# Starting the FFN on two batches and re-timing loads in a fused retention and SwiGLU kernel

## The chip, the cores and the metric

One core of one Trainium2 chip. The metric is the device time of one execution in microseconds. The profile's span is about 1.7 us shorter than that time. TensorE is called PE in the profile, its weight loads PEld, VectorE DVE, ScalarE ACT, GpSimd POOL, SyncE SP. SPq is SyncE's sequencer, which does nothing here but issue DMAs. The "landing" of a DMA is the moment its data has arrived; landing times are counted from the start of the issue. A line of a timeline holds start, length, engine, line, operation, output and input.

## The reference, cut to what matters

Retention attention over 4 batches, 8 heads, 768 positions, head size 64, then RMS norm and a SwiGLU FFN (512 to 1536 to 512) over the 3072 tokens.

```
for t in range(S):                       # retention
    state = gamma * state + k[t] v[t]^T
    y[t]  = scale * q[t] state
xn  = x / sqrt(mean(x*x) + 1e-6) * rms_g # FFN
out = (silu(xn @ w_gate) * (xn @ w_val)) @ w_out
```

## The kernel before: the parts that matter

The positions are cut into 6 chunks of 128. FFN group c works on chunk c of all four batches (512 tokens), while the attention of chunk c+1 is woven into its slots: slots 0 to 11 are the gate and value products ("gv"), the later ones the down products ("down"). The order of the program is each engine's order; there is no scheduler.

In what follows, b is the batch, and xn is the normalised x of one batch and chunk; group c's first full product needs the transposes of all four xn of chunk c. For chunks 2 and later q, k and the normalised xn are transposed by DMA, all issued from SyncE:

```
def piece_t(c, b):                 # T: transposes of q and k
    if c > 1:
        for n in "qk":
            t = work.tile([128, NHP, 128], BF16, name=n + "T", bufs=8)
            nc.sync.dma_start_transpose(out=t, in_=d[n + "b"])
        return
    ...                            # chunks 0 and 1: on TensorE

def piece_n(c, b):                 # N: normalised x
    if c > 1:
        nc.vector.scalar_tensor_tensor(out=xn, in0=x, scalar=d["rstd"], in1=g_bc, ...)
        nc.sync.dma_start_transpose(out=cur[c, "xnT"][:, :, b * C:(b + 1) * C], in_=xn)
        return
    ...
```

The slots of a group, and what is done ahead for the chunk after next (L load, T transposes, V the product v times decay):

```
PLAN = dict(a=(5, 5, 9, 9), y=(7, 8, 11, 12), n=(9, 10, 13, 13))   # chunks 2..5
AHEAD = {1: ((L, 0),), 3: ((L, 1),), 5: ((L, 2),), 7: ((T, 0),), 8: ((T, 1),), 9: ((L, 3),), 11: ((T, 2),),
         13: ((V, 0),), 14: ((V, 1), (T, 3)), 15: ((V, 2), (V, 3))}
for c in range(NCH):
    for i, f_slot in enumerate(ffn(c)):
        f_slot()                          # gv(i), or down(b): 12 products, a copy, an output DMA on SyncE
        for f in a_slots[i]: f()          # the attention of chunk c+1, by PLAN
        ahead(c, i)                       # the work for chunk c+2, by AHEAD
```

Of the kernel before, what the change touches and what calls it, by code (L numbers as in the profile page):

```python
# [9 lines left out]
F32 = mybir.dt.float32  # L10
# [7 lines left out]
def kernel(  # L18
# [11 lines left out]
    nc = tc.nc  # L30
# [31 lines left out]
            nc.sync.dma_start(out=x, in_=src[0].rearrange("h (c p) d -> c p h d", p=C)[0])  # L62
            raw[name] = x

    def load(c, b):
        d = cur.setdefault((c, b), {})
        for name, src in (("qb", q), ("kb", k)):
            x = work.tile([128, DM], BF16, name=name, bufs=8)
            nc.gpsimd.dma_start(  # L69
                out=x.rearrange("p (h d) -> p h d", h=H),  # L70
                in_=src[b].rearrange("h (c p) d -> c p h d", p=C)[c])
            d[name] = x
        d["v_f"] = loads.tile([128, H, D], F32, name="v_f")
        nc.gpsimd.dma_start(out=d["v_f"], in_=v[b].rearrange("h (c p) d -> c p h d", p=C)[c])  # L74

    cur = {}
    load_first()
# [42 lines left out]
    nc.vector.memset(mhalf, -0.5)  # L120
    ident = const.tile([128, 128], BF16, name="ident")
    make_identity(nc, ident)
    for b in range(1, B):
        load(0, b)

    g_bc = const.tile([128, DM], F32, name="g_bc")
# [12 lines left out]
    wg_v = moe_w_gate.rearrange("(k p) n -> p k n", p=128)  # L139
    wv_v = moe_w_val.rearrange("(k p) n -> p k n", p=128)  # L140
    wo_v = moe_w_out.rearrange("(n p) m -> p n m", p=128)
    WB = ((0, 384), (384, 768), (768, DFF))

    def load_wg(i):
        sl = slice(*WB[i])
# [19 lines left out]
    def piece_c(b):  # L165
# [3 lines left out]
            copy(d[name], raw[name[0] + "_f"].rearrange("p h d -> p (h d)"))  # L169
        d["v_f"] = raw["v_f"]  # L170

    def piece_v(c, b):
        d = cur[c, b]
        d["vp"] = work.tile([128, H, D], BF16, name="vp", bufs=6)
        (nc.vector if c == 0 and b < 3 else nc.gpsimd).tensor_tensor(  # L175
            out=d["vp"], in0=d["v_f"], in1=vdec[:, c, :, None].to_broadcast([128, H, D]), op=ALU.mult)

    def piece_t(c, b):
# [37 lines left out]

    def piece_y(c, b):
        d = cur[c, b]
        pool, tag = (fps, "ff") if c == 0 else (aps, "at")
        y_ps = pool.tile([128, H, D], F32, name="y_ps", tag=tag)  # L220
        first = True
        for hp in range(NHP):
            for i in range(2):
                h = 2 * hp + i
                last = c == 0 and h == H - 1
                nc.tensor.matmul(y_ps[:, h, :], d["am"][:, i, hp, :], d["vp"][:, h, :],  # L226
                                 start=first, stop=last, skip_group_check=True)
                first = False
        if c > 0:
            for hp in range(NHP):  # L230
                nc.tensor.matmul(y_ps[:, 2 * hp:2 * hp + 2, :], d["qT"][:, hp, :], st_b[b][:, hp, :],  # L231
                                 start=False, stop=hp == NHP - 1, skip_group_check=True)
        if 0 < c < NCH - 1:
            kv_ps = piece_kv(c, b)
        x = y_ps if c == 0 else work.tile([128, H, D], F32, name="x", bufs=5)
        if c > 0:
            nc.vector.tensor_tensor(  # L237
                out=x, in0=y_ps, in1=ydec[:, c, :, None].to_broadcast([128, H, D]), op=ALU.mult)
        xsq = work.tile([128, DM], F32, name="xsq", bufs=1)
        ssq = work.tile([128, 1], F32, name="ssq")  # L240
        nc.scalar.activation(xsq, x.rearrange("p h d -> p (h d)"), AF.Square,  # L241
                             accum_out=ssq)
        d["ssq"] = ssq
        d["x"] = x
        if c == 0:
            return
        piece_rstd(c, b)
        if c < NCH - 1:
            nc.vector.tensor_tensor(out=st_f[b], in0=st_f[b], in1=kv_ps, op=ALU.add)
            piece_sb(b)  # L250

    def piece_kv(c, b):
        d = cur[c, b]
# [7 lines left out]
    def piece_s(b):  # L261
        nc.scalar.copy(st_f[b], piece_kv(0, b))

    def piece_sb(b):
        for i in range(2):
            r = slice(i * 64, i * 64 + 64)
            nc.gpsimd.tensor_copy(st_b[b][r, :, i * 64:i * 64 + 64], st_f[b][r, :, i * 64:i * 64 + 64])  # L267

    def piece_rstd(c, b):
        ms = work.tile([128, 1], F32, name="ms")  # L270
# [18 lines left out]
    def piece_x(c, b):  # L289
        d = cur[c, b] if c == 0 else cur.pop((c, b))  # L290
        if c > 1:
            return
        xn = d["xn"]
        xt_ps = aps.tile([128, KS, 128], BF16, name="xt_ps", tag="at")
        for s in range(KS):
            nc.tensor.transpose(xt_ps[:, s, :], xn[:, s * 128:(s + 1) * 128], ident)  # L296
        xnT = cur[c, "xnT"][:, :, b * C:(b + 1) * C]
        if c == 0 and b < 2:
            for s in range(KS):
                nc.scalar.activation(xnT[:, s, :], xt_ps[:, s, :], AF.Copy, scale=g_col[:, s:s + 1])  # L300
            return
        nc.vector.tensor_tensor(  # L302
            out=xnT, in0=xt_ps,
            in1=g_col[:, :, None].to_broadcast([128, KS, 128]), op=ALU.mult)
# [5 lines left out]

    PLAN = dict(a=(5, 5, 9, 9), y=(7, 8, 11, 12), n=(9, 10, 13, 13))

    PLAN1 = dict(v=(7, 9, 11, 14), t=(8, 10, 12, 15), a=(9, 11, 14, 17), y=(10, 13, 16, 19), n=(12, 15, 18, 21), x=(13, 17, 20, 22))

    def attention(c):
        s = [[] for _ in range(24 if c == 1 else 16)]
        s[0].append(lambda: begin(c))
        plan = PLAN1 if c == 1 else PLAN
        pieces = dict(v=piece_v, t=piece_t, a=piece_a, y=piece_y, n=piece_n, x=piece_x)
        for b in range(B):  # L320
            for n, slot in plan.items():
                s[slot[b]].append(lambda f=pieces[n], b=b: f(c, b))
        return s


    def ffn(c):
# [2 lines left out]
        slots = []  # L329


        def gv(n0, n1=None, t=slice(0, GT)):
            n1 = n0 + 1 if n1 is None else n1
            w = t.stop - t.start
            g_ps = fps.tile([128, n1 - n0, w], F32, name="g_ps", tag="ff")
            v_ps = fps.tile([128, n1 - n0, w], F32, name="v_ps", tag="ff")
            for ps, w_b in ((g_ps, wg_b), (v_ps, wv_b)):
                for n in range(n0, n1):
                    for s in range(KS):
                        nc.tensor.matmul(ps[:, n - n0, :], w_b[:, s, n * 128:(n + 1) * 128], xnT[:, s, t],  # L340
                                         start=s == 0, stop=s == KS - 1)
            sg = ffw.tile([128, n1 - n0, w], BF16, name="sg")
            nc.scalar.activation(sg, g_ps, AF.Silu)  # L343
            nc.vector.tensor_tensor(out=hT[:, n0:n1, t], in0=sg, in1=v_ps, op=ALU.mult)  # L344


        EARLY = 4
        early = slice(0, GT - C)

        def gv_first(n):  # L350
            gv(n, t=early)
            if n == 1:
                piece_x(0, B - 1)
            if n == EARLY - 1:
                gv(0, EARLY, slice(GT - C, GT))

        o_t = {}

# [22 lines left out]
            nc.sync.dma_start(out=out_v[c, b], in_=o_sb)  # L381

        for n in range(NFF):
            slots.append(lambda n=n: gv_first(n) if c == 0 and n < EARLY else gv(n))
        if c == 0:
            for i in range(3):
                for b in range(B):
# [11 lines left out]
    def warm_up(c, n):  # L399
        for i in range(n):  # L400
            nc.tensor.matmul(hot_ps, hot[:, 0:128], hot, start=True, stop=True)  # L401

    P = dict(C=lambda c, b: piece_c(b), V=piece_v, T=piece_t, A=piece_a, Y=piece_y,
             R=piece_rstd, N=piece_n, X=piece_x, G=lambda c, i: load_wg(i), U=lambda c, i: load_wv(i), H=warm_up)
    for step in ("H9 H8 C0 T0 H4 V0 A0 H4 V1 T1 H4 G0 Y0 R0 U0 H4 A1 V2 T2 H4 Y1 R1 G1 U1 H2 A2 N0 T3 Y2 R2 "
                 "X0 N1 H2 A3 X1 N2 H9 H6 X2 H3 V3 Y3 H6 G2 U2 R3 N3").split():
        P[step[0]](0, int(step[1]))
    make_causal()
    load(1, 0)

    L, T, V, W = load, piece_t, piece_v, lambda c, i: load_wo(i)
    AHEAD = {1: ((L, 0),), 3: ((L, 1),), 5: ((L, 2),), 7: ((T, 0),), 8: ((T, 1),), 9: ((L, 3),), 11: ((T, 2),),
             13: ((V, 0),), 14: ((V, 1), (T, 3)), 15: ((V, 2), (V, 3))}


    AHEAD0 = {2: ((L, -1, 1),), 4: ((W, 0),), 5: ((L, -1, 2),), 6: ((W, 1),), 8: ((L, -1, 3),), 9: ((W, 2), (L, 0)),
              11: ((L, 1),), 13: ((T, 0),), 14: ((L, 2),), 15: ((T, 1),), 19: ((T, 2), (L, 3))}
    LATE0 = {0: ((V, 0), (V, 1), (V, 2)), 1: ((T, 3),), 4: ((V, 3),)}

    def ahead(c, i):  # L420
        for f, *x in (AHEAD0 if c == 0 else AHEAD).get(i, ()) if c < NCH - 2 else ():
            f(c + 2 + sum(x[:-1]), x[-1])
        for f, b in LATE0.get(i, ()) if c == 1 else ():
            f(2, b)

    for c in range(NCH):
        f_slots = ffn(c)
        a_slots = attention(c + 1) if c + 1 < NCH else [[] for _ in range(16)]
        for i, f_slot in enumerate(f_slots):
            if i == NFF + 1 and c > 0:  # L430

                for f in a_slots[i]:
                    f()
                a_slots[i] = []
            f_slot()
            if c == 0 and i < B:
                piece_s(i)
                piece_sb(i)
            for f in a_slots[i]:
                f()  # L440
            ahead(c, i)
            if c == 0 and i == 22:
                nc.sync.dma_start(out=g_bc, in_=moe_rms_g.partition_broadcast(128))
# [1 line left out]
_INS = ['q', 'k', 'v', 'moe_w_gate', 'moe_w_val', 'moe_w_out', 'moe_rms_g']  # L445
# [26 lines left out]
```

## Time and profile before

| | before |
|---|---|
| time | 237.49 us (237.37 to 237.71, 3 runs) |
| first FFN product | 20.43 us |
| group 1 starts | 61.67 us |
| group 2 starts | 96.80 us |
| TensorE busy from 61.67 to 221.80 us | 159.07 of 160.13 us |

Here is SyncE's timeline in group 1 (start, length of the issue, engine, line, operation, output and input):

```profile
73.54 1.19 SPq L183 DMA_TRANSPOSE qT<-qb  x1
74.82 1.22 SPq L183 DMA_TRANSPOSE kT<-kb  x1
77.00 1.20 SPq L183 DMA_TRANSPOSE qT<-qb  x1
78.28 1.22 SPq L183 DMA_TRANSPOSE kT<-kb  x1
83.11 4.81 SPq L284 DMA_TRANSPOSE xnT<-xn  x2
88.02 1.22 SPq L183 DMA_TRANSPOSE qT<-qb  x1
89.33 1.22 SPq L183 DMA_TRANSPOSE kT<-kb  x1
90.64 1.09 SPq L381 DMA_DIRECT2D out_dram<-o_sb  x1
91.82 2.53 SPq L284 DMA_TRANSPOSE xnT<-xn  x2
```

Two pairs of q and k transposes are issued before the first xn is ready, and one pair stands between the second and the third transpose of xn. The answer for the last two transposes of xn, and TensorE's timeline where group 2 wants them:

```profile
DMA to landing us min/median/max: 2.5/2.5/2.5
```

```profile
96.80 1.03 PE L340 MATMUL g_ps<-xnT,wg_b 128*128 128x512 bf16 x4
```

The last of them lands at 95.61 us. So the kernel before had a margin of 1.2 us there, and no row of a page says so. VectorE had the third and fourth xn ready at 91.1 and 92.7 us, so each was issued within 0.8 us.

### The profile page before, as it was taken

To read this page: it belongs to the slowest core of one execution; us is meant where nothing else is said; L and a number is where in the kernel's file an instruction comes from. 1 tells how busy PE (TensorE), PEld (TensorE's weight loads), DVE (VectorE), ACT (ScalarE), POOL (GpSimd) and SP (SyncE) were. 2 spreads that over 40 slices of the span, in tenths; PEclk is the share of its full clock that TensorE was granted. 3 is DMA by queue.
4 is the path that set the end of the run, shared out by engine and by line. 5 is a ranking of instruction groups with operands and counts; after the bars stand their busy time and mean duration, and the time that the engine had idled before them with its cause. 6 is when DMAs were issued, how large, how long until landed. Compare 5 with 4: busy or idle time off the path is not lost.

```text
span 236.0 us, 4231 instructions
## 1 busy us (share of the span) xinstructions
PE 226.4 (96%) x1587; PEld 119.3 (51%) x1613; DVE 126.8 (54%) x212; ACT 88.9 (38%) x172; POOL 128.5 (54%) x198
## 2 busy tenths in 40 slices
PE   7979999999899999999999999999999999999994
PEld 4657744565345555445554445554445554444443
DVE  6585435678337794147794147794148582243300
ACT  7475544432433423333433333433332532433221
POOL 8978989887997458970458970559300202000000
PEclk9999999999999999999999999999999999999999
DMA  7999999999999998899099999695900025200022
GB/s 135 178 188 204 211 193 204 206 196 139 180 271 174 163 139 152 172 213 161 11 127 122 173 205 104 79 133 135 181 0 0 3 44 152 73 0 0 0 89 90
DMA packets 87956, 30.69 MB, mean 130 GB/s; under 512 B 78528, under 2 KB 83392, under 8 KB 87936
## 3 DMA queue, kind: packets, MB, share of 16 engines
q0 software_dynamic: 54432, 16.78, 70.9%
q1 hardware_dynamic: 32832, 13.51, 30.7%
q8 instruction: 12, 0.20, 0.4%
q10 hardware_dynamic: 672, 0.13, 0.3%
q14 instruction: 8, 0.07, 0.1%
HBM read 28.58 MB, written 6.29 MB: 148 GB/s over the span
## 4 chain that ended last, share of the span: by engine, by line
PE 85%; DVE 4%; ACT 4%; POOL 3%; issue 2%; ACTq 0%; DVEq 0%; POOLq 0%
PE g_ps L340 26%; PE v_ps L340 26%; PE o_ps L375 21%; PE a_ps L208 3%; PE y_ps L226 2%; PE hot_ps L401 2%; PE y_ps L231 2%; PE kv_ps L257 2%; DVE am L214 1%; DVE xn L286 1%; PE o_ps L365 1%; ACT xsq L241 1%; DVE x L237 1%; PE xt_ps L296 1%; POOL rstd L274 1%
## 5 line engine op out<-in xcount | busy, mean ns | idle before, releaser
L344 DVE TENSOR_TENSOR hT<-sg,v_ps 128x512 bf16<-128x512 bf16 (+1 forms) x73 | 49.5, 678 | 79.9 <-PE v_ps L340 70.0
L340 PE MATMUL v_ps<-xnT,wv_b 128*128 128x512 bf16 (+2 forms) x298 | 73.5, 368 | 0.4
L340 PE MATMUL g_ps<-xnT,wg_b 128*128 128x512 bf16 (+2 forms) x293 | 73.1, 368 | 0.5
L343 ACT ACTIVATE sg<-g_ps 128x512 bf16<-128x512 f32 (+1 forms) x73 | 43.0, 589 | 64.8 <-PE g_ps L340 62.4
L375 PE MATMUL o_ps<-wo_b,hT 128*128 128x512 bf16 x267 | 61.9, 379 | 0.5 <-issue 0.2
L340 PEld LDWEIGHTS <-wv_b 128*128 128x128 bf16 x304 | 29.1, 98 | 33.1
L340 PEld LDWEIGHTS <-wg_b 128*128 128x128 bf16 x304 | 27.7, 98 | 29.2 <-DVE xnT L302 0.4
L375 PEld LDWEIGHTS <-hT 128*128 128x128 bf16 x276 | 26.1, 98 | 28.7 <-DVE hT L344 0.2
L271 POOL TENSOR_SCALAR ms<-ssq 128x1 f32<-128x1 f32 x24 | 5.6, 232 | 62.3 <-ACT xsq L241 61.9
L241 ACT ACTIVATE xsq<-x 128x512 f32<-128x512 f32 x20 | 12.6, 630 | 35.1 <-DVE x L237 33.3
L214 DVE TENSOR_TENSOR am<-a_ps,causal 128x512 bf16<-128x512 f32 x40 | 24.9, 679 | 0.0
L380 ACT COPY o_sb<-o_ps 128x512 f32<-128x512 f32 x23 | 13.2, 581 | 29.3 <-PE o_ps L375 23.3
L69 POOL DMA_DIRECT2D qb<-in_q_dram x23 | 21.7, 944 | 0.4 <-DMA kb<-in_k_dram 0.3
L175 POOL TENSOR_TENSOR vp<-v_f,vdec 128x512 bf16<-128x512 f32 x21 | 21.5, 1042 | 0.5
L74 POOL DMA_DIRECT2D v_f<-in_v_dram x23 | 21.3, 924 | 0.1
L69 POOL DMA_DIRECT2D kb<-in_k_dram x23 | 20.7, 901 | 0.1
L267 POOL CAST st_b<-st_f 64x256 bf16<-64x256 f32 x40 | 18.1, 454 | 1.3
L237 DVE TENSOR_TENSOR x<-y_ps,ydec 128x512 f32<-128x512 f32 x20 | 13.7, 684 | 2.9 <-PE y_ps L231 2.9
L282 DVE SCALAR_TENSOR_TENSOR xn<-x,rstd,g_bc 128x512 bf16<-128x512 f32 x16 | 12.7, 791 | 3.5 <-POOL rstd L274 3.5
L274 POOL TENSOR_TENSOR rstd<-ms,mhalf 128x1 f32<-128x1 f32 x24 | 13.3, 555 | 2.0
L401 PE MATMUL hot_ps<-hot 128*128 128x256 bf16 x65 | 11.6, 329 | 1.1 <-DVE hot L93 1.1
L226 PEld LDWEIGHTS <-am 128*128 128x128 bf16 x192 | 8.8, 98 | 5.3 <-DVE am L214 0.9
(71 smaller groups left out, 145.5 us busy)
## 6 DMA issues: line engine op xcount, KB each, us to landing
v_f<-in_v_dram POOLq DMA_DIRECT2D x23, 256.0 KB, 7.3
out_dram<-o_sb SPq DMA_DIRECT2D x23, 256.0 KB, 2.3
qb<-in_q_dram POOLq DMA_DIRECT2D x23, 128.0 KB, 7.1
kb<-in_k_dram POOLq DMA_DIRECT2D x23, 128.0 KB, 6.8
wo_b<-in_moe_w_out_dram POOLq DMA_DIRECT2D x3, 512.0 KB, 9.7
wg_b<-in_moe_w_gate_dram POOLq DMA_DIRECT2D x2, 384.0 KB, 6.5
wv_b<-in_moe_w_val_dram POOLq DMA_DIRECT2D x2, 384.0 KB, 7.3
wg_b<-in_moe_w_gate_dram POOLq DMA_DIRECT2D x1, 768.0 KB, 8.6
```

The source lines that it names most:

```text
L69: nc.gpsimd.dma_start(out=x.rearrange("p (h d) -> p h d", h=H), in_=src[b].rearrange("h (c p) d -> c p h d", p=C)[c])
L74: nc.gpsimd.dma_start(out=d["v_f"], in_=v[b].rearrange("h (c p) d -> c p h d", p=C)[c])
L175: (nc.vector if c == 0 and b < 3 else nc.gpsimd).tensor_tensor(out=d["vp"], in0=d["v_f"], in1=vdec[:, c, :, None].to_broadcast([128, H, D] ...
L214: nc.vector.tensor_tensor(out=am[:, i], in0=a_ps[i], in1=mask, op=ALU.mult)
L237: nc.vector.tensor_tensor(out=x, in0=y_ps, in1=ydec[:, c, :, None].to_broadcast([128, H, D]), op=ALU.mult)
L267: nc.gpsimd.tensor_copy(st_b[b][r, :, i * 64:i * 64 + 64], st_f[b][r, :, i * 64:i * 64 + 64])
L274: nc.gpsimd.tensor_tensor(out=rstd, in0=ms, in1=mhalf, op=ALU.pow)
L340: nc.tensor.matmul(ps[:, n - n0, :], w_b[:, s, n * 128:(n + 1) * 128], xnT[:, s, t], start=s == 0, stop=s == KS - 1)
L343: nc.scalar.activation(sg, g_ps, AF.Silu)
L344: nc.vector.tensor_tensor(out=hT[:, n0:n1, t], in0=sg, in1=v_ps, op=ALU.mult)
L375: nc.tensor.matmul(o_ps, hT[:, n, b * C:(b + 1) * C], wo_b[:, n, :], start=n == 0, stop=n == NFF - 1)
L401: nc.tensor.matmul(hot_ps, hot[:, 0:128], hot, start=True, stop=True)
```

## The change

Its intent: start the FFN on two batches as soon as they are normalised, with the weights loaded ahead of the fourth batch; let group 1 start on three batches; take state copies and some products off GpSimd; load chunk 2 within group 0. The core of the diff (the head's order of steps and helper functions are cut, some lines joined, comments added):

```diff
-    WB = ((0, 384), (384, 768), (768, DFF))
+    WB = tuple((i * 384, (i + 1) * 384) for i in range(4))
+    VECTOR_V = ((0, 0), (0, 1), (0, 2), (1, 1), (1, 2), (1, 3))      # V on VectorE for these
-            piece_sb(b)
+            piece_sb(b, nc.gpsimd.tensor_copy if c > 1 else nc.scalar.copy)
+        def first(i):                       # group 0: two batches, then three, the fourth later
+            two, three, third, fourth = slice(0, 2 * C), slice(0, 3 * C), slice(2 * C, 3 * C), slice(3 * C, GT)
+            if i == 0:
+                gv(0, 2, two, lambda: piece_x(0, 2)); gv(2, 3, two); gv(0, 3, third)
+            elif i < 8:
+                gv(i + 2, t=three)
+            ...
+        def second(n):                      # group 1: three batches for its first two gates
+            gv(n, t=slice(0, GT - C))
+            ...
 ... (cut)
+    AHEAD0 = {1: ((L, 1, 1),), 5: ((W, 0, 0),), 6: ((L, 1, 2),), ...    # group 0: chunk 1, w_out, chunk 2
+              16: ((L, 2, 3, "qk"),), 17: ((L, 2, 3, "v"),), 23: ((T, 2, 2),)}
+    AHEAD1 = {0: ((V, 1, 0), (V, 1, 1), (V, 1, 2)), 1: ((T, 1, 3),), 3: ((V, 1, 3),),
+              4: ((L, 2, 0),), 6: ((L, 2, 1),), 8: ((L, 2, 2),), 9: ((T, 2, 0), (L, 2, 3)), 11: ((T, 2, 1),),
+              12: ((T, 2, 2),), 13: ((V, 2, 0),), 14: ((V, 2, 1), (T, 2, 3)), 15: ((V, 2, 2), (V, 2, 3))}
```

Group 1 gets a plan of its own, AHEAD1. Its second number is relative to the group, so (L, 2, 0) and (T, 2, 0) are chunk 3's batch 0. Against AHEAD, chunk 3's loads go from slots 1, 3, 5, 9 to 4, 6, 8, 9, and its transposes from 7, 8, 11, 14 to 9, 11, 12, 14.

More of the change, by code (lines that the diff above doesn't have):

```diff
@@ L63, in load_first, with load @@
             raw[name] = x
-    def load(c, b):
+    def load(c, b, parts="qkv"):
         d = cur.setdefault((c, b), {})
-        for name, src in (("qb", q), ("kb", k)):
-            x = work.tile([128, DM], BF16, name=name, bufs=8)
-            nc.gpsimd.dma_start(
-                out=x.rearrange("p (h d) -> p h d", h=H),
-                in_=src[b].rearrange("h (c p) d -> c p h d", p=C)[c])
-            d[name] = x
-        d["v_f"] = loads.tile([128, H, D], F32, name="v_f")
-        nc.gpsimd.dma_start(out=d["v_f"], in_=v[b].rearrange("h (c p) d -> c p h d", p=C)[c])
+        for n in parts:
+            if n == "v":
+                x = d["v_f"] = loads.tile([128, H, D], F32, name="v_f")
+            else:
+                d[n + "b"] = work.tile([128, DM], BF16, name=n + "b", bufs=8)
+                x = d[n + "b"].rearrange("p (h d) -> p h d", h=H)
+            nc.gpsimd.dma_start(out=x, in_=dict(q=q, k=k, v=v)[n][b].rearrange("h (c p) d -> c p h d", p=C)[c])
     cur = {}
@@ L122 @@
     make_identity(nc, ident)
-    for b in range(1, B):
+    for b in (1, 2):
         load(0, b)
@@ L174, in piece_v @@
         d["vp"] = work.tile([128, H, D], BF16, name="vp", bufs=6)
-        (nc.vector if c == 0 and b < 3 else nc.gpsimd).tensor_tensor(
+        (nc.vector if (c, b) in VECTOR_V else nc.gpsimd).tensor_tensor(
             out=d["vp"], in0=d["v_f"], in1=vdec[:, c, :, None].to_broadcast([128, H, D]), op=ALU.mult)
@@ L218, in piece_y @@
         d = cur[c, b]
-        pool, tag = (fps, "ff") if c == 0 else (aps, "at")
+        pool, tag = (fps, "ff") if c == 0 and b < B - 1 else (aps, "at")
         y_ps = pool.tile([128, H, D], F32, name="y_ps", tag=tag)
@@ L262, in piece_s, with piece_sb @@
         nc.scalar.copy(st_f[b], piece_kv(0, b))
-    def piece_sb(b):
+    def piece_sb(b, copy=nc.scalar.copy):
         for i in range(2):
             r = slice(i * 64, i * 64 + 64)
-            nc.gpsimd.tensor_copy(st_b[b][r, :, i * 64:i * 64 + 64], st_f[b][r, :, i * 64:i * 64 + 64])
+            copy(st_b[b][r, :, i * 64:i * 64 + 64], st_f[b][r, :, i * 64:i * 64 + 64])
     def piece_rstd(c, b):
@@ L297, in piece_x @@
         xnT = cur[c, "xnT"][:, :, b * C:(b + 1) * C]
-        if c == 0 and b < 2:
+        if (c, b) == (0, 0):
             for s in range(KS):
@@ L311 @@
     PLAN = dict(a=(5, 5, 9, 9), y=(7, 8, 11, 12), n=(9, 10, 13, 13))
-    PLAN1 = dict(v=(7, 9, 11, 14), t=(8, 10, 12, 15), a=(9, 11, 14, 17), y=(10, 13, 16, 19), n=(12, 15, 18, 21), x=(13, 17, 20, 22))
+    PLAN1 = dict(v=(9, 12, 14, 17), t=(9, 11, 13, 16), a=(10, 12, 15, 18), y=(11, 14, 17, 20),
+                 n=(13, 16, 19, 22), x=(15, 18, 21, None))
     def attention(c):
@@ L319, in attention @@
         pieces = dict(v=piece_v, t=piece_t, a=piece_a, y=piece_y, n=piece_n, x=piece_x)
-        for b in range(B):
-            for n, slot in plan.items():
-                s[slot[b]].append(lambda f=pieces[n], b=b: f(c, b))
+        for n, slot in plan.items():
+            for b in range(B):
+                if slot[b] is not None:
+                    s[slot[b]].append(lambda f=pieces[n], b=b: f(c, b))
         return s
@@ L329, in ffn, with gv @@
         slots = []
-        def gv(n0, n1=None, t=slice(0, GT)):
+        def gv(n0, n1=None, t=slice(0, GT), between=None):
             n1 = n0 + 1 if n1 is None else n1
@@ L337, in gv @@
             for ps, w_b in ((g_ps, wg_b), (v_ps, wv_b)):
+                if between is not None and ps is v_ps:
+                    between()
                 for n in range(n0, n1):
@@ L344, in gv @@
             nc.vector.tensor_tensor(out=hT[:, n0:n1, t], in0=sg, in1=v_ps, op=ALU.mult)
-        EARLY = 4
-        early = slice(0, GT - C)
-        def gv_first(n):
-            gv(n, t=early)
-            if n == 1:
-                piece_x(0, B - 1)
-            if n == EARLY - 1:
-                gv(0, EARLY, slice(GT - C, GT))
+        def first(i):
+            two, three, third, fourth = slice(0, 2 * C), slice(0, 3 * C), slice(2 * C, 3 * C), slice(3 * C, GT)
+            if i == 0:
+                gv(0, 2, two, lambda: piece_x(0, 2))
+                gv(2, 3, two)
+                gv(0, 3, third)
+            elif i < 8:
+                gv(i + 2, t=three)
+            else:
+                gv(*((0, 4), (4, 8), (8, 10), (11, 12))[i - 8], fourth if i < 11 else slice(0, GT))
+                if i == 10:
+                    gv(10)
+            for f, *x in {1: ((piece_s, 0),), 2: ((piece_t, 0, 3), (piece_s, 1)), 3: ((piece_a, 0, 3),),
+                          4: ((piece_s, 2), (piece_y, 0, 3), (piece_rstd, 0, 3)), 5: ((piece_n, 0, 3), (piece_s, 3)),
+                          6: ((piece_x, 0, 3), (piece_sb, 0)), 7: ((piece_sb, 1),), 8: ((piece_sb, 2),),
+                          9: ((piece_sb, 3),)}.get(i, ()):
+                f(*x)
+        def second(n):
+            gv(n, t=slice(0, GT - C))
+            if n == 0:
+                piece_x(1, B - 1)
+            else:
+                gv(0, 2, slice(GT - C, GT))
         o_t = {}
@@ L383, in ffn @@
         for n in range(NFF):
-            slots.append(lambda n=n: gv_first(n) if c == 0 and n < EARLY else gv(n))
+            slots.append(lambda n=n: first(n) if c == 0 else second(n) if c == 1 and n < 2 else gv(n))
         if c == 0:
@@ L403 @@
     P = dict(C=lambda c, b: piece_c(b), V=piece_v, T=piece_t, A=piece_a, Y=piece_y,
-             R=piece_rstd, N=piece_n, X=piece_x, G=lambda c, i: load_wg(i), U=lambda c, i: load_wv(i), H=warm_up)
-    for step in ("H9 H8 C0 T0 H4 V0 A0 H4 V1 T1 H4 G0 Y0 R0 U0 H4 A1 V2 T2 H4 Y1 R1 G1 U1 H2 A2 N0 T3 Y2 R2 "
-                 "X0 N1 H2 A3 X1 N2 H9 H6 X2 H3 V3 Y3 H6 G2 U2 R3 N3").split():
+             R=piece_rstd, N=piece_n, X=piece_x, G=lambda c, i: load_wg(i), U=lambda c, i: load_wv(i), H=warm_up,
+             **{n: lambda c, b, n=n: load(c, b, n) for n in "qkv"})
+    for step in ("H9 H8 C0 T0 H4 V0 A0 H4 V1 T1 H4 G0 U0 Y0 G1 U1 R0 H4 A1 V2 T2 H4 q3 Y1 R1 k3 H2 A2 H6 N0 Y2 R2 v3 "
+                 "H2 X0 N1 H3 X1 N2 H6 G2 U2 G3 U3").split():
         P[step[0]](0, int(step[1]))
@@ L409 @@
     load(1, 0)
+    piece_v(0, 3)
     L, T, V, W = load, piece_t, piece_v, lambda c, i: load_wo(i)
-    AHEAD = {1: ((L, 0),), 3: ((L, 1),), 5: ((L, 2),), 7: ((T, 0),), 8: ((T, 1),), 9: ((L, 3),), 11: ((T, 2),),
-             13: ((V, 0),), 14: ((V, 1), (T, 3)), 15: ((V, 2), (V, 3))}
-    AHEAD0 = {2: ((L, -1, 1),), 4: ((W, 0),), 5: ((L, -1, 2),), 6: ((W, 1),), 8: ((L, -1, 3),), 9: ((W, 2), (L, 0)),
-              11: ((L, 1),), 13: ((T, 0),), 14: ((L, 2),), 15: ((T, 1),), 19: ((T, 2), (L, 3))}
-    LATE0 = {0: ((V, 0), (V, 1), (V, 2)), 1: ((T, 3),), 4: ((V, 3),)}
+    AHEAD = {1: ((L, 2, 0),), 3: ((L, 2, 1),), 5: ((L, 2, 2),), 7: ((T, 2, 0),), 8: ((T, 2, 1),), 9: ((L, 2, 3),),
+             11: ((T, 2, 2),), 13: ((V, 2, 0),), 14: ((V, 2, 1), (T, 2, 3)), 15: ((V, 2, 2), (V, 2, 3))}
+    AHEAD0 = {1: ((L, 1, 1),), 5: ((W, 0, 0),), 6: ((L, 1, 2),), 8: ((W, 0, 1),), 9: ((L, 1, 3),),
+              10: ((W, 0, 2), (L, 2, 0)), 12: ((L, 2, 1),), 13: ((T, 2, 0),), 14: ((L, 2, 2),), 15: ((T, 2, 1),),
+              16: ((L, 2, 3, "qk"),), 17: ((L, 2, 3, "v"),), 23: ((T, 2, 2),)}
+    AHEAD1 = {0: ((V, 1, 0), (V, 1, 1), (V, 1, 2)), 1: ((T, 1, 3),), 3: ((V, 1, 3),),
+              4: ((L, 2, 0),), 6: ((L, 2, 1),), 8: ((L, 2, 2),), 9: ((T, 2, 0), (L, 2, 3)), 11: ((T, 2, 1),),
+              12: ((T, 2, 2),), 13: ((V, 2, 0),), 14: ((V, 2, 1), (T, 2, 3)), 15: ((V, 2, 2), (V, 2, 3))}
     def ahead(c, i):
-        for f, *x in (AHEAD0 if c == 0 else AHEAD).get(i, ()) if c < NCH - 2 else ():
-            f(c + 2 + sum(x[:-1]), x[-1])
-        for f, b in LATE0.get(i, ()) if c == 1 else ():
-            f(2, b)
+        for f, dc, *x in {0: AHEAD0, 1: AHEAD1}.get(c, AHEAD).get(i, ()) if c < NCH - 2 else ():
+            f(c + dc, *x)
     for c in range(NCH):
@@ L435 @@
             f_slot()
-            if c == 0 and i < B:
-                piece_s(i)
-                piece_sb(i)
             for f in a_slots[i]:
@@ L441 @@
             ahead(c, i)
-            if c == 0 and i == 22:
+            if c == 1 and i == 4:
                 nc.sync.dma_start(out=g_bc, in_=moe_rms_g.partition_broadcast(128))
```

## The prediction

> **What bounds the kernel now.** I read the page's busy row first, then the windows of each engine, then TensorE's timeline, then GpSimd's, and last the issues of transfers.
>
> ```profile
> PE 226.4 (96%) x1587; PEld 119.3 (51%) x1613; DVE 126.8 (54%) x212; ACT 88.9 (38%) x172; POOL 128.5 (54%) x198
> ```
>
> TensorE (PE) is the bound on average, but the share hides stages. The windows view cut at the moments where the work changes (columns: length of stretch, then busy time and instruction count of PE, PEld, DVE, ACT, POOL, then clock, DMA share, GB/s):
>
> ```profile
> 0.00:20.43 20.43, 17.18 (x174) 12.20 (x174) 13.99 (x36) 12.81 (x26) 18.12 (x31) 1.00 1.38 172
> 20.43:40.00 19.57, 19.46 (x150) 11.43 (x150) 7.99 (x13) 9.71 (x18) 17.94 (x28) 1.00 1.50 200
> 40.00:61.67 21.67, 20.02 (x189) 11.32 (x191) 16.19 (x27) 8.35 (x16) 18.71 (x31) 1.00 1.62 186
> 61.67:221.80 160.13, 159.07 (x1021) 78.55 (x1041) 87.50 (x135) 55.78 (x109) 73.71 (x110) 1.00 0.91 114
> ```
>
> From 61.67 us, where group 1 of the FFN starts, TensorE has practically no gap (159.07 of 160.13, and some records are missing): nothing can be won there. What can be won lies before 61.67 us: a head of 20.43 us in which TensorE is "busy" largely with warm-up products of zeros, and 1.65 us of gaps between 40 and 61.67. The timeline of TensorE at the end of the head and at the end of group 0:
>
> ```profile
> 17.11 1.80 PE L401 MATMUL hot_ps<-hot 128*128 128x256 bf16 x15
> 18.98 0.40 PE L296 MATMUL xt_ps<-ident,xn 128*128 128x128 bf16 x4
> 19.21 0.49 PE L401 MATMUL hot_ps<-hot 128*128 128x256 bf16 x3
> 19.54 0.40 PE L226 MATMUL y_ps<-vp,am 128*128 128x64 bf16 x8
> 19.77 0.82 PE L401 MATMUL hot_ps<-hot 128*128 128x256 bf16 x6
> 20.43 0.81 PE L340 MATMUL g_ps<-xnT,wg_b 128*128 128x384 bf16 x4
> ...
> 60.49 0.40 PE L296 MATMUL xt_ps<-ident,xn 128*128 128x128 bf16 x4 [0.87 <-DVE xn L286]
> ```
>
> 24 warm-ups fill the time in which the third batch's normalisation is awaited. The last line is the longest wait of group 0: the transposition of batch 3 before group 1. GpSimd's timeline shows why the chains ahead of it run late:
>
> ```profile
> 52.10 1.04 POOL L175 TENSOR_TENSOR vp<-v_f,vdec 128x512 bf16<-128x512 f32 x1
> 53.09 0.97 POOL L69 DMA_DIRECT2D qb<-in_q_dram  x1
> 54.06 0.89 POOL L69 DMA_DIRECT2D kb<-in_k_dram  x1
> 54.93 0.92 POOL L74 DMA_DIRECT2D v_f<-in_v_dram  x1
> 55.92 0.19 POOL L271 TENSOR_SCALAR ms<-ssq 128x1 f32<-128x1 f32 x1
> 56.19 0.56 POOL L274 TENSOR_TENSOR rstd<-ms,mhalf 128x1 f32<-128x1 f32 x1
> ```
>
> ScalarE had the sum of squares ready at 54.2; the rstd waited 1.7 us behind a product and three load issues.
>
> **What the Trainium skill says.** "DMA: Bandwidth & Descriptors", § SWDGE vs HWDGE vs iDMA: a load that casts can only be issued from GpSimd, whose cores write the descriptors, and all queues share the same 16 engines. The trace agrees: an issue holds GpSimd for 0.75 to 0.97 us. "GPSIMD Engine Reference", § 4.1 Engine selection: a two-input elementwise operation is about twice as slow there as on VectorE. Here the product vp takes 1.042 us on GpSimd and 0.689 on VectorE, a factor of 1.5. "TensorE: Matmul & The Clock Gate", § Back-to-back issue gap: a warm product of N columns issues every N/2.4 + 2.5 ns alone, 216 ns at 512; the trace's four products in 0.865 us agree. § Part 1 explains the warm-ups (an idle array runs at half clock); the after kernel keeps 56 of 65, so I expect the clock at 1.00 as now.
>
> **The change part by part.** I take starts from rows of the trace, so all durations are spacings seen there: four products of 512 columns 0.865 us, of 384 0.65, of 256 0.43 (half of 0.865), of 128 0.22; eight transposes 0.445; scores (a) 0.33; y 0.23; y with state 0.45; kv 0.22.
>
> Head. Up to the masking of batch 2 (ends 15.20) nothing in the order changes on TensorE, VectorE or ScalarE. Then VectorE normalises batches 0 and 1 back to back (15.20 to 16.60, now as before). Their transposes follow at 16.0 and 16.65. Batch 0 is scaled on ScalarE, which is free at about 16.3 since the copy for batch 3 is gone: four pieces, half of the 2.17 us that eight took, end at 17.45. Batch 1 goes to VectorE: 16.95 + 0.68 = 17.65. So the first FFN product starts at about 17.7 instead of 20.43: **2.7 us earlier**. But batch 3's transposes (0.445), scores (0.33) and y (0.23), and batch 2's normalised transpose (0.22), leave the head and now lie on TensorE's path: 1.23 us. Net 1.5. Splitting group 0 into pieces of 256, 384 and 128 columns costs little: 24 x 0.1075 + 24 x 0.0557 + 7 x 1.30 + 2 x 2.225 + 2 x 1.73 = 20.9 us, against 8 x 0.65 + 1.78 + 8 x 1.73 = 20.8.
>
> Do the weights come in time? The quarters are 0.79 MB each at the source. Before, the first halves' landings (issue plus landing time) are 17.4, 19.7, 21.7, 23.6 us and the two double-sized ones 27.3 and 31.4: about 2 us a piece, DMA engines over 90% busy. If the queue is limited by bytes, the after order lands the same number of bytes at the same time: wg0 15, wv0 17.4, wg1 19.5, wv1 21.7, then batch 3, wg2 25.5, wv2 27.3, wg3 29.4, wv3 31.4. Laying the products end to end from 17.7, they are wanted at 17.7, 18.8, 21.9, 22.5, and 27.0, 27.65, 31.8, 32.4. All hold, wv2 by 0.3 us only.
>
> Group 0, second half. TensorE's work from FFN start to group 1 is, before: gates and values 20.8, kv of chunk 0 0.9, five transposes of xn 1.1, chunk 1's transposes 1.8, scores 1.3, y and kv 2.7, down 48 x 0.2165 = 10.4, sum 39.0, against 41.24 elapsed: 2.2 us of gaps. After: 20.9 + 0.9 + 1.1 (still five: two of chunk 0, three of chunk 1) + 1.0 (batch 3's transposes, scores and y) + 1.8 + 1.3 + 2.7 + 10.4 = 40.1. With no gap group 1 starts at 57.8; then the 0.25 us that the last transposition and the narrow pieces cost there.
>
> What closes the gaps: on GpSimd, 16 state copies (6.6 us in this stage) go to ScalarE, and three products vp (3.1 us) to VectorE; loads are placed so that rstd stands free. I laid the chains of chunk 1 by hand: VectorE gets four pairs of masks (1.25 each), x, state sums and vp (0.6 each, 11 of them), xnT and xn (0.6), about 16.5 us of the 17.7 us from the tenth gate to group 1. It goes from three quarters to over 90% in this stretch, so some waits of 0.05 to 0.3 us remain on TensorE: I allow 0.3 to 0.5 in sum. ScalarE gets 16 copies at about 0.37 us (estimate from its 128x256 copy): 6 us, on an engine that had half its time free.
>
> Sum: 61.67 - (57.8 + 0.25 + 0.4) = 3.2 us; from 61.67 on the same work without gaps, so it reaches the end. 237.49 - 3.2 = 234.3; I say 234.4, a ratio of 1.013.
>
> **The rivals.** (1) Weights late: for it, DMA share at the top and a margin of 0.3 us for wv2; against, the same bytes in the same order landed in time before. A slip of 1 us in each of the two last value quarters makes 235.5. (2) VectorE becomes the bound between 40 and 58 us, with the late batches' x and xn queueing on it: for it, over 90%; against, group 1 now starts with three batches, which gives the fourth 1.3 us more. Half the gaps stay: 235.4. (3) GpSimd still blocks: each load waits until the one eight before it has landed, and the key load of chunk 2's last batch stands before the third rstd; I place its issue at 53.4 to 54.3, the squares ready at 53.5. The loss is under 1 us. (4) The head gains less because the wait moves from batch 2 to the transposes of batch 0 and 1, which I counted; if batch 2's normalisation (17.65 to 18.35, wanted at 18.6) is late, up to 0.5 us. (5) Everything fits without a gap: 233.7.
>
> **Range and chances.** Most rivals cost 0.5 to 1 us and could come together: 233.5 to 235.9. Two per cent is 4.75 us; even with no gap at all I find 3.8. So faster by over 2% 0.04, within 2% 0.94, slower 0.02.
>
> **What would show it.** The first FFN product near 17.7; group 1's first full product near 58.4; 56 warm-ups; no wait for transfers by gate or value products; VectorE over 90% from 40 to 58; GpSimd's busy sum in 20 to 62 lower by some 6 us or more; after group 1's start the same length to the end as before, about 174.3 us. Wrong would be: a first product at 19 or later, a gap before a value product at 27 to 33, or a longer stretch after group 1.

## The result, and the profile after

The changed kernel took 248.22 us (246.57 to 249.58, 4 runs) against 237.60 of the kernel before. The ratio is 1.044 (95% interval 1.036 to 1.053): 4.4% slower. The profiled run is the one of 246.91 us. Here and below a ratio is the mean time of one kernel's fast runs over that of the other's fast runs of the same rounds, so not quite the ratio of the medians quoted.

The windows view of the changed kernel, cut at the same events as the prediction's (same columns):

```profile
0.00:17.91 17.91, 14.87 (x137) 9.83 (x138) 12.10 (x34) 10.44 (x20) 15.19 (x28) 1.00 1.30 171
17.91:59.09 41.18, 40.92 (x437) 27.72 (x438) 27.76 (x47) 25.34 (x53) 33.99 (x47) 1.00 1.64 195
59.09:94.63 35.54, 35.54 (x261) 18.51 (x259) 22.15 (x35) 12.54 (x27) 25.01 (x36) 1.00 1.34 164
94.63:103.94 9.31, 0.00 (x1) 0.03 (x1) 0.00 (x0) 0.59 (x1) 8.04 (x10) 0.70 1.59 161
```

The first FFN product starts at 17.91 (predicted 17.7). TensorE is busy for 40.92 of the next 41.18 us. Group 1 starts at 59.09 and its last product ends at 94.63, 2.2 us earlier than before's 96.80. Then TensorE does nothing for 9.31 us, and the granted clock falls to 0.70. TensorE's timeline there:

```profile
86.70 7.93 PE L397 MATMUL o_ps<-wo_b,hT 128*128 128x512 bf16 x36
103.94 1.87 PE L346 MATMUL g_ps<-xnT,wg_b 128*128 128x512 bf16 x4 [9.31 <-DMA out_dram<-o_sb]
105.60 1.91 PE L346 MATMUL v_ps<-xnT,wv_b 128*128 128x512 bf16 x4
```

The groups of four products (one line of the timeline each) then start 1.66, 1.71 and 1.47 us after one another in place of 0.865: 4.84 - 2.60 = 2.2 us more. From group 2's start to the end of the span it takes 141.3 us (245.2 - 103.9) in place of 139.2 (236.0 - 96.8), 2.1 us more, which these three groups account for within 0.1 us. The account closes: -2.2 (earlier end of group 1) + 9.3 (gap) + 2.1 (after it) = +9.2, and the spans are 245.2 and 236.0. It is the account of this run; two of the four runs took 249.5 us, 2.6 us more, and were not profiled, so where they lost that is open. "Cold" below means at half of the full clock.

The wait is put down to an output DMA. That is the releaser the profile infers last, and it is the wrong one: the gate product reads xnT, and the trace's landing of the last transpose of xn is 103.69 us (issued at 97.08, 6.6 us). The output that shares its time is no input of it. SyncE's timeline shows why the transpose was issued so late:

```profile
68.69 0.57 SPq L465 DMA_DIRECT2D g_bc<-in_moe_rms_g_dram  x1
83.16 1.20 SPq L286 DMA_TRANSPOSE xnT<-xn  x1
84.45 1.22 SPq L185 DMA_TRANSPOSE qT<-qb  x1
85.76 1.29 SPq L185 DMA_TRANSPOSE kT<-kb  x1
87.14 1.30 SPq L286 DMA_TRANSPOSE xnT<-xn  x1
88.54 1.22 SPq L185 DMA_TRANSPOSE qT<-qb  x1
89.84 2.57 SPq L185 DMA_TRANSPOSE kT<-kb  x1
92.51 0.53 SPq L403 DMA_DIRECT2D out_dram<-o_sb  x1
93.13 1.22 SPq L185 DMA_TRANSPOSE qT<-qb  x1
94.44 1.22 SPq L185 DMA_TRANSPOSE kT<-kb  x1
95.76 2.62 SPq L286 DMA_TRANSPOSE xnT<-xn  x2
```

From 69.3 to 83.16 SyncE stands idle: q and k of chunk 3's first batch had landed by 75.7 and those of its second by 78.1, but in the new order their transposes come after the first transpose of xn, which waits for VectorE. From 83.16 on SyncE issues without a pause. The four transposes that used to be done at 73 to 79 now stand between those of xn: 1.22 + 1.29 + 1.22 + 2.57 = 6.3 us of issue. VectorE had the third and fourth xn ready at 88.7 and 90.3; they were issued at 95.76 and 97.08. And once issued they took two to 2.7 times as long as before:

```profile
DMA to landing us min/median/max: 5.0/5.8/6.6
```

This is the answer for these two transposes in the changed kernel, against 2.5 before. Chunk 4's loads had begun on GpSimd at 94.66, ahead of them; before, they began at 96.99, after them.

### The profile page after: what moved, and what is told of

It reads as the page before. It is cut to its first block, busy times and chain, and to the rows that moved or that the text cites. A ratio compares the mean times of both kernels' runs of the same rounds, so it can differ in the third digit from the quotient of the medians.

```text
span 245.2 us, 4432 instructions
## 1 busy us (share of the span) xinstructions
PE 229.3 (94%) x1692; PEld 123.5 (50%) x1692; DVE 129.9 (53%) x219; ACT 94.3 (38%) x187; POOL 120.0 (49%) x181
## 4 chain that ended last, share of the span: by engine, by line
PE 86%; DMA 4%; POOL 2%; SPq 2%; DVE 2%; ACT 1%; issue 1%; POOLq 0%; DVEq 0%; ACTq 0%
PE g_ps L346 26%; PE v_ps L346 25%; PE o_ps L397 23%; PE a_ps L210 2%; DMA out_dram<-o_sb 2%; DMA kb<-in_k_dram 2%; PE y_ps L228 2%; PE y_ps L233 2%; PE kv_ps L259 2%; PE qk_ps L199 1%; PE o_ps L387 1%; SPq L286 1%; SPq L185 1%; PE xt_ps L298 1%; POOL qb L73 1%
## 5 line engine op out<-in xcount | busy, mean ns | idle before, releaser
L350 DVE TENSOR_TENSOR hT<-sg,v_ps 128x512 bf16<-128x512 bf16 (+2 forms) x76 | 50.0, 657 | 89.4 <-PE v_ps L346 79.3
L346 PE MATMUL g_ps<-xnT,wg_b 128*128 128x512 bf16 (+3 forms) x348 | 76.3, 347 | 9.5 <-DMA out_dram<-o_sb 9.3
L346 PE MATMUL v_ps<-xnT,wv_b 128*128 128x512 bf16 (+3 forms) x348 | 75.6, 345 | 0.0
L349 ACT ACTIVATE sg<-g_ps 128x512 bf16<-128x512 f32 (+2 forms) x76 | 43.6, 573 | 75.8 <-PE g_ps L346 74.8
L397 PE MATMUL o_ps<-wo_b,hT 128*128 128x512 bf16 x276 | 62.7, 379 | 0.0
L346 PEld LDWEIGHTS <-wg_b 128*128 128x128 bf16 x348 | 30.4, 99 | 37.7 <-issue 11.9
L346 PEld LDWEIGHTS <-wv_b 128*128 128x128 bf16 x348 | 31.9, 98 | 31.5 <-issue 1.3
L177 POOL TENSOR_TENSOR vp<-v_f,vdec 128x512 bf16<-128x512 f32 x18 | 18.5, 1052 | 4.4 <-DMA v_f<-in_v_dram 4.2
L423 PE MATMUL hot_ps<-hot 128*128 128x256 bf16 x56 | 10.6, 338 | 1.1 <-DVE hot L92 1.1
L269 POOL CAST st_b<-st_f 64x256 bf16<-64x256 f32 x24 | 10.5, 437 | 0.7
```

The costliest lines, as they stand in the source:

```text
L177: (nc.vector if (c, b) in VECTOR_V else nc.gpsimd).tensor_tensor(out=d["vp"], in0=d["v_f"], in1=vdec[:, c, :, None].to_broadcast([128, H, ...
L346: nc.tensor.matmul(ps[:, n - n0, :], w_b[:, s, n * 128:(n + 1) * 128], xnT[:, s, t], start=s == 0, stop=s == KS - 1)
L349: nc.scalar.activation(sg, g_ps, AF.Silu)
L350: nc.vector.tensor_tensor(out=hT[:, n0:n1, t], in0=sg, in1=v_ps, op=ALU.mult)
L397: nc.tensor.matmul(o_ps, hT[:, n, b * C:(b + 1) * C], wo_b[:, n, :], start=n == 0, stop=n == NFF - 1)
```

## The experiments

Theory A: SyncE issues in program order, and the foreign transposes between those of xn make the last xn late; the landing time and the cold clock follow from the lateness. Rival B: the DMA engines are crowded because the change issues chunk 3's loads later. Rival C: any faster group 1 runs into an xn chain that does not move with it. All kernels below gave correct results. "Slow" on a single core means only that a run was over 1.5% above the fastest of the same kernel.

### 1. The order on SyncE undone

```diff
-              ... 8: ((L, 2, 2),), 9: ((T, 2, 0), (L, 2, 3)), 11: ((T, 2, 1),),
+              ... 7: ((T, 2, 0),), 8: ((L, 2, 2), (T, 2, 1)), 9: ((L, 2, 3),),
```

> The changed kernel, with only the transposing DMAs of chunk 3's batches 0 and 1 put back ahead of group 1's transposes of xn on SyncE (slots 7 and 8 instead of 9 and 11). Theory A (SyncE issues its DMAs in order, and four foreign transposes of 1.2 to 2.6 us each stand between the second and the third transposes of xn, so the last xn lands 9 us late): the 9.3 us gap before group 2 vanishes, with it the cold products after it, and the time is 234 to 235.5. Theory B (the DMA engines are crowded by chunk 3's loads, which the change issues later): the gap stays at 6 us or more, time 243 or more.

236.51 us (235.83 to 237.11), ratio 0.995. Moving four DMA issues took back 11.7 us of the medians (248.22 - 236.51). The clock was 0.998. A gap of 0.97 us before group 2 remained: the first xn transposes landed 6.4 and 7.4 us after issue, and the last at 96.31, where the down products had ended at 95.4. So A names the main cause, but the gap did not vanish and the time is above A's range by 1 us; this profile also shows 1.1 us of waits for a value weight in group 0.

### 2. The loads moved back, the order left

```diff
-              ... 1: ((T, 1, 3),), 3: ((V, 1, 3),),
+              ... 1: ((L, 2, 0), (T, 1, 3)), 3: ((L, 2, 1), (V, 1, 3)), 5: ((L, 2, 2),),
-              4: ((L, 2, 0),), 6: ((L, 2, 1),), 8: ((L, 2, 2),), 9: ((T, 2, 0), (L, 2, 3)), ...
+              9: ((T, 2, 0), (L, 2, 3)), ...
```

> The changed kernel, with chunk 3's loads back at slots 1, 3, 5 and 9 of group 1 and its transposing DMAs left where the change put them. Theory A: the order on SyncE is unchanged, so the gap before group 2 stays within 1.5 us of 9.3 and the time at 245 to 249. Theory B (late loads crowd the DMA engines): the gap falls by half or more, time 242 or less.

243.54 us (242.81 to 244.25), ratio 1.024. The longest wait of TensorE:

```profile
PE g_ps L346 <- DMA xnT<-xn: 5.9, 1, 5.9
```

It lies between the two theories' ranges: with this order of transposes the late loads cost some 3.4 us of the gap, so B holds for a part, and most of the gap stays.

### 3. Only the order, put into the kernel before

```diff
-            f(c + 2 + sum(x[:-1]), x[-1])
+            if c != 1 or f is not T:
+                f(c + 2 + sum(x[:-1]), x[-1])
+        for b in {9: (0,), 11: (1,), 12: (2,), 14: (3,)}.get(i, ()) if c == 1 else ():
+            T(3, b)
```

> The kernel before, with only the transposing DMAs of chunk 3 moved to where the change has them (slots 9, 11, 12, 14 of group 1). Theory A: a gap of 5 to 10 us before group 2 and a cold clock after it, time 243 to 249. Theory B or any theory that needs the rest of the change: 237 to 238.5.

240.91 us (239.99 to 241.87), ratio 1.013. The direction is A's, the size is under half of what I expected: the profiled run, the fastest of the four, kept its clock (0.998) and has this wait before group 2:

```profile
PE g_ps L340 <- DMA xnT<-xn: 2.3, 1, 2.3
```

Against the changed kernel's 9.3 us that is 7.0 us less, and the traces account for it. Group 1 ends 2.2 us later here (96.82 against 94.63), the last xn is issued 0.7 us earlier (96.35 against 97.08), and it lands 2.5 us after issue in place of 6.6, 4.1 us less: chunk 4's loads began at 96.84, behind it. So the order alone, without the rest of the change, makes a loss; a gain upstream lengthens the wait, and so does the collision with chunk 4's loads. Two of the other three runs have lower clocks (0.985 and 0.993) and were not profiled.

### 4. The gap filled with warm-ups

```diff
+            if c == 1 and i == 15:
+                hot_ps2 = aps.tile([128, 256], F32, name="hot_ps2", tag="at")
+                for _ in range(80):
+                    nc.tensor.matmul(hot_ps2, hot[:, 0:128], hot, start=True, stop=True)
```

> The changed kernel with 80 warm-up products of zeros (0.11 us each, 8.8 us) after the last slot of group 1, which fill the gap without removing its cause. Theory A with a share for the clock: the last xn lands as late as before, but group 2's first three product groups take 0.87 instead of 1.4 to 1.7 us each, so the time falls by 2 to 2.6 us to about 244.5. If the clock had no part: unchanged, 246.5 to 249.

246.19 us (244.33 to 246.70), ratio 1.034 against the changed kernel's 1.044, which is 2.4 us; but the two intervals overlap (1.030 to 1.038, 1.036 to 1.053), so the traces decide. The last xn lands at 105.11, 1.4 us later than in the changed kernel, and a wait of 2.3 us is left. From group 2's start to the end it takes 139.0 us (244.4 - 105.4) in place of 141.3, as in the kernel before (139.2). The windows after the gap, in the changed kernel and then here:

```profile
103.90:110.00 6.10, 6.06 (x18) 2.34 (x19) 0.78 (x2) 1.19 (x2) 0.00 (x0) 0.62 1.70 197
```

```profile
104.00:110.00 6.00, 4.58 (x21) 2.18 (x23) 1.38 (x2) 1.32 (x3) 0.00 (x0) 1.00 1.35 236
```

The clock column goes from 0.62 to 1.00. The Trainium skill, "TensorE: Matmul & The Clock Gate", § Part 1, says that an idle window of about 3.4 us drops the array to half clock. These runs agree only in part. Gaps of 1.0 and 2.3 us left the mean clock at 0.998, gaps of 4.4, 4.7, 5.9 and 9.3 us were each followed by half clock (means of 0.986, 0.986, 0.986 and 0.979). But near the skill's figure the length of the gap does not decide. In experiment 7 a gap of 2.7 us, from 57.77 to 60.44, was followed by half clock:

```profile
61.70:65.10 3.40, 3.40 (x13) 1.44 (x11) 2.64 (x5) 1.69 (x4) 2.81 (x6) 0.50 1.18 171
```

And in experiment 5 a second gap, of 3.9 us, was not:

```profile
140.89:146.00 5.11, 5.06 (x23) 2.34 (x25) 1.38 (x2) 1.79 (x3) 5.11 (x7) 1.00 1.30 178
```

### 5. Chunk 4's loads out of the way

Group 2 got a plan with its loads at slots 7 to 10, behind its first rstd on GpSimd, and its transposes behind all of xn:

```diff
+    AHEAD2 = {7: ((L, 2, 0),), 8: ((L, 2, 1),), 9: ((L, 2, 2),), 10: ((L, 2, 3),), 13: ((V, 2, 0),),
+              14: ((V, 2, 1), (T, 2, 0), (T, 2, 1), (T, 2, 2)), 15: ((V, 2, 2), (V, 2, 3), (T, 2, 3))}
```

> The changed kernel with chunk 4's loads, which run into the last two transposes of xn, issued behind group 2's first rstd instead, and chunk 4's transposing DMAs after group 2's transposes of xn. It sizes one part: in the changed kernel these two landed 5.0 and 6.6 us after issue, in the one before 2.5. If the loads cause that: landing 2.5 to 3.5, the gap before group 2 falls from 9.3 to 5 to 6.5 us, time 242 to 244.5. If SyncE's order alone counts: landing still 5 or more, time unchanged at 246 to 249.

247.20 us (246.41 to 249.81), ratio 1.044: the time did not move, as I had expected only for the case that the order alone counts, but the gap in question did. The landing of the last two transposes of xn, and TensorE's longest wait:

```profile
DMA to landing us min/median/max: 2.5/2.5/2.5
```

```profile
PE g_ps L346 <- DMA xnT<-xn: 8.3, 2, 4.4
```

Landing is 2.5 us as expected for the other case, and the gap before group 2 is 4.4 us in place of 9.3, even less than the 5 to 6.5 I gave. Of the difference 4.1 us are the landing (2.5 in place of 6.6). The rest comes from the last xn being issued 1.0 us earlier (96.07 against 97.08), and that is not the moved loads: 0.8 us of it is one transpose of k at 89.7 that held SyncE for 1.78 us in place of 2.57, before any load of chunk 4. So of 9.3 us about 4.1 are the collision with chunk 4's loads, which only a late transpose meets, and about 5.2 the lateness of the issue. The 3.4 us of experiment 2 overlap with these two shares and do not add to them. The second of the two waits, 3.9 us before group 3, is of my making: the moved loads now ran into group 2's xn. A collision moved is not a collision removed.

### 6. The whole plan of group 1 as before

Loads at 1, 3, 5, 9 and transposes at 7, 8, 11, 14, the rest of the change kept.

> The changed kernel with the whole of group 1's plan for chunk 3 as before (loads at slots 1, 3, 5, 9; transposing DMAs at 7, 8, 11, 14), everything else of the change kept. Theory A2 (the loss is SyncE's order first, and chunk 3's later loads crowding the transposes of xn second; the rest of the change works as predicted): no gap of over 0.5 us before group 2, last xn landed before the last down product ends, time 234 to 235.5. Theory C (any faster start of group 1 meets an xn chain that does not move with it, so the gain turns into a wait): a gap of 1.5 us or more remains, time 236.5 to 238.

A miss. Four runs gave 237.17 us once and 242.40 to 242.92 three times; the three count as slow, and no ratio was formed. The profiled run was one of the three: a wait of 4.7 us for xnT. In it chunk 3's loads were issued from 61.5 us on (66.4 in the kernel before), while outputs and chunk 2's transposes were still in flight, and took up to 17.9 us to land, against 11.2 at most for chunk 3's first three batches before; the transposes on SyncE waited for them and reached the time of xn again. As only slow runs were seen from inside, I take from this no more than a suspicion: the old slots do not fit the new, faster GpSimd safely.

### 7. Copies and products back on GpSimd

On top of the restored plan:

```diff
-            piece_sb(b, nc.gpsimd.tensor_copy if c > 1 else nc.scalar.copy)
+            piece_sb(b)                                   # always GpSimd
-    VECTOR_V = ((0, 0), (0, 1), (0, 2), (1, 1), (1, 2), (1, 3))
+    VECTOR_V = ((0, 0), (0, 1), (0, 2))
-    def piece_sb(b, copy=nc.scalar.copy):
+    def piece_sb(b, copy=nc.gpsimd.tensor_copy):
```

> The restored plan with the state copies of chunks 0 and 1 and the three products vp of chunk 1 back on GpSimd; only this part of the change undone. If moving them off GpSimd was what closed the gaps of group 0's second half: group 1 starts 1 us or more later than in the restored plan and the time is 1 to 2 us longer, 235 to 237. If the placing of the loads and the start of group 1 on three batches did it: within 0.5 us of the restored plan.

240.91 us (239.65 to 241.70), ratio 1.013. TensorE's longest wait:

```profile
PE y_ps L228 <- POOL vp L177: 4.4, 2, 2.7
```

Group 1 starts at 65.61 us against 58.78 in the restored plan's profile (that run counts as slow, but its loss comes later; experiment 8's profile has 58.91). This part of the change is worth 6.8 us up to there, far more than the 1 to 2 I gave it. The two waits are 4.4 us of that, and about 1.7 us is the half clock after the second one (an estimate: the 16 products between 61.12 and 65.61 take 4.5 us, and 2.8 at the spacings seen elsewhere). The reason, argued from the rows and not tested apart: with chunk 2's loads inside group 0, GpSimd could not have carried the copies and products as well.

### 8. All of chunk 3's transposes later still, but behind xn

The decisive one. The changed kernel's loads untouched; T of all four batches at slots 14 and 15:

```diff
-              4: ((L, 2, 0),), 6: ((L, 2, 1),), 8: ((L, 2, 2),), 9: ((T, 2, 0), (L, 2, 3)), 11: ((T, 2, 1),),
-              12: ((T, 2, 2),), 13: ((V, 2, 0),), 14: ((V, 2, 1), (T, 2, 3)), 15: ((V, 2, 2), (V, 2, 3))}
+              4: ((L, 2, 0),), 6: ((L, 2, 1),), 8: ((L, 2, 2),), 9: ((L, 2, 3),), 13: ((V, 2, 0),),
+              14: ((V, 2, 1), (T, 2, 0), (T, 2, 1)), 15: ((V, 2, 2), (V, 2, 3), (T, 2, 2), (T, 2, 3))}
```

> The changed kernel, its loads untouched, with all transposing DMAs of chunk 3 moved behind all four transposes of xn on SyncE: later still than the change put them, but no longer between the transposes of xn. If lateness of these transposes or the load on the DMA engines made the loss: a gap of 5 us or more stays, time 243 or more. If their place between the transposes of xn made it: last xn lands by 95.5, gap under 1 us, time 234.5 to 236.5.

235.51 us (234.84 to 236.67), ratio 0.991. SyncE and TensorE around the end of group 1:

```profile
82.97 2.53 SPq L286 DMA_TRANSPOSE xnT<-xn  x2
86.70 0.33 SPq L403 DMA_DIRECT2D out_dram<-o_sb  x1
88.58 2.94 SPq L286 DMA_TRANSPOSE xnT<-xn  x2
```

```profile
86.52 7.93 PE L397 MATMUL o_ps<-wo_b,hT 128*128 128x512 bf16 x35
94.38 1.02 PE L346 MATMUL g_ps<-xnT,wg_b 128*128 128x512 bf16 x4
```

The third xn is issued at 88.58 in place of 95.76 and there is no gap. The transposes of chunk 3 are later than in the changed kernel and harm nothing but a wait of 0.5 us in group 2. So neither their lateness nor that of the loads makes the gap by itself: their place between the transposes of xn does, and the loads then lengthen it. The margin is thin here: the last xn lands at 94.24, 0.14 us before it is wanted. Rival C falls too. VectorE had the third xn of chunk 2 ready at 88.7 us in the changed kernel and at 91.1 in the one before: the chain of xn does move with group 1.

### 9. Versions that use this

(a) The restored plan, with the third and fourth batch's transposes behind all of xn in every group (11 to 14, 14 to 15):

> The same as the restored plan, and in every group the transposing DMAs of the third and fourth batch stand behind all four transposes of xn, so that nothing foreign but one output stands between them on SyncE. Theory A2: as the restored plan or up to 0.5 us faster, 233.7 to 235, the last xn of each group landing earlier. Theory C: no change against the restored plan.

Fast runs 234.67, 235.26 and 235.36 us, ratio 0.989; one run of 245.56. That one was not profiled, and what happened in it stays open.

(b) The changed kernel's load slots, first two pairs at slots 7 and 8, the others behind xn in every group:

```diff
+              4: ((L, 2, 0),), 6: ((L, 2, 1),), 7: ((T, 2, 0),), 8: ((L, 2, 2), (T, 2, 1)), 9: ((L, 2, 3),),
+              13: ((V, 2, 0),), 14: ((V, 2, 1), (T, 2, 2)), 15: ((V, 2, 2), (V, 2, 3), (T, 2, 3))}
```

> The changed kernel with its own load slots, chunk 3's first two transposing pairs ahead of the transposes of xn (slots 7, 8), and in every group the third and fourth pairs behind them. It lets the idle SyncE of 69 to 83 us do the first pairs and leaves nothing foreign between the transposes of xn. Theory A: 234.3 to 235.8, no run above 237.5. If the loads of chunk 3 issued late (81 to 86 us) crowd xn by themselves: a gap of 1 us or more, 236 to 238.

235.26 us (235.20 to 235.73), ratio 0.990, no gap before group 2. In this profile TensorE waited 1.0 us for a value weight in group 0.

(c) As (b), with the second load at slot 4 and the third at slot 6:

> As the previous one, with chunk 3's third load ahead of group 1's first rstd on GpSimd (slot 6) and the second at slot 4, so that only the fourth load runs into the transposes of xn. If late loads crowd xn: 0.5 to 1 us faster than the previous one and its first two xn land within 5 us of issue instead of 6.4 to 7.4. If loads issued early crowd instead, as in the restored plan: slower than the previous one by 1 us or more, or with runs 5 us longer.

235.48 us (234.66 to 237.09), ratio 0.992. Its first two xn landed 5.3 and 4.5 us after issue, against 5.4 and 5.9 in (b): the second fits the expectation, the time does not show it.

(d) The program of (b) again:

> The same program as the version with the first pairs early and xn first, in five rounds, to narrow its interval and to see whether a slow execution with a gap before group 2 ever occurs: ratio to the kernel before 0.988 to 0.992, no execution above 237.5.

235.03 us (234.84 to 235.26, 4 runs), ratio 0.989 (interval 0.988 to 0.991). It beats both kernels, by 1.1% and by about 5.3% of the medians, and none of the eight executions of this program, here and in (b), took more than 235.8 us; the two profiled ones have no gap before group 2. In its trace the last xn lands at 92.96 us, 1.1 us before group 2 wants it at 94.09.

## Why the prediction was wrong, point by point

- **First product near 17.7**: 17.91. Right.
- **Net 1.5 us from the head, weights in time**: in the profiled run no product waited for a weight; two other runs with the same head showed waits of about 1 us (experiments 1 and 9b). The margin of 0.3 us was rightly called thin.
- **Group 1's first full product near 58.4**: 59.09 for the three-batch product that comes first, plus the 0.25 us that I had counted. The gain at this point is 61.67 - 59.34 = 2.3 us, not 3.2. I had summed 40.1 us of work from the first product; 41.18 elapsed, 1.1 us more where I allowed 0.3 to 0.5 us of waits. A term mis-sized. Only 0.26 us of that shows as idle time; the rest lies in products spaced a little wider than the spacings that I summed, and what held them is open.
- **VectorE over 90% from 40 to 58**: 16.26 of 18.00 us. Right, at the edge, and it was no bound.
- **GpSimd's busy sum in 20 to 62 lower by 6 us or more**: 34.71 against 37.26, lower by 2.6. The copies did leave, but GpSimd, now free, took up work from after 62 (three products of chunk 2, 3.2 us from 58.68 on), and chunk 0's product for batch 3 (1.1 us) and one more value load (0.9 us) now fall into this stretch. I had counted what leaves and not what moves in.
- **Moving copies and products is worth a share of 2 us**: experiment 7 shows 6.8 us up to group 1, as it carries the earlier loads of chunk 2 as well.
- **"from 61.67 on the same work without gaps, so it reaches the end"**: this is the step that failed. The stretch had no gap because its inputs landed 1.2 us before they were wanted; I read the absence of gaps as the absence of limits. In place of a passed-on gain the runs showed a new wait of 9.3 us, of which about 5.2 us is the late issue on SyncE and about 4.1 us the collision with loads (experiment 5), plus 2.1 to 2.3 us of cold clock (experiment 4). Moving nothing but the transposes of q and k takes away all but 1.0 us of the wait (experiment 1) or all of it (experiment 8). My own sign of being wrong came true: from group 1's start to the end it took 186.1 us (245.2 - 59.09), not 174.3.
- **The rivals**: none of the five named SyncE. The working never costed the new plan of group 1, although the diff shows it: chunk 3's transposes move across those of xn on an in-order queue. My three engines were the ones the page has rows for; SyncE has no row in its busy part.
- **Two per cent is out of reach as a gain**: no run here reached it. With the order mended the change gives 1.1%, 235.03 us, which lies within the range that I gave for the change as it stood (233.5 to 235.9).

What stays open: why the old load slots (experiment 6) gave two kinds of execution, the one slow run of 9a, and the 2.6 us between the changed kernel's two faster and two slower runs.

## What to carry to other kernels

A stretch without gaps has a margin, not a guarantee: before passing an upstream gain through it, look up when its last input landed and when it was wanted. When work is re-slotted, write down the new order of every queue that issues in order, the DMA issuers too, and ask which entry that is not yet ready now stands ahead of which that is. Keep transfers that gate the bottleneck engine next to one another in such a queue, and put the patient ones before or behind them all.

## What the Trainium skill lacked or had wrong

- "DMA: Bandwidth & Descriptors", § Issuing engines are not separate DMA queues, says that issuing from several engines saves only sequencer time, "which is usually small relative to the DMA itself". Here it was not small: one transpose held SyncE for 1.2 to 2.6 us, four of them for 6.3 us, while the transposes of xn in the kernel before landed 2.5 us after issue.
- No page gives the landing time of a transposing DMA beside other traffic: the last two transposes of xn landed 2.5 us after issue in the kernel before, where the loads ahead of them had landed, and 5.0 and 6.6 us after issue in the changed one, among chunk 4's loads.
- "TensorE: Matmul & The Clock Gate", § Part 1: its figure of about 3.4 us is no limit for the length of one gap. Half clock followed a gap of 2.7 us (experiment 7) and not one of 3.9 us (experiment 5).
